# Weight decode and one of two r products moved to GpSimd in a fused recurrence and MLP kernel, with a refitted order of work

## The chip, the core and the metric

One NeuronCore of one Trainium2 chip runs the whole program. The metric is the device time of one execution in microseconds. Engines are named as in the profile: PE is TensorE, PEld its weight loads, DVE is VectorE, ACT is ScalarE, POOL is GpSimd, SP is SyncE, which issues nearly all DMAs.

## What is computed

A gated linear recurrence over 768 steps (4 batches, 8 heads of width 48) is followed by a two-layer MLP whose gate is a clipped parabola.

```python
for t in range(S):                      # S = 768
    cur = einsum('bhd,bhe->bhde', u[None] * kt, vt)
    y[:, :, t] = einsum('bhd,bhde->bhe', rt, state + cur)
    state = wt[:, :, :, None] * state + einsum('bhd,bhe->bhde', kt, vt)
x = y.transpose(0, 2, 1, 3).reshape(3072, 384)
h = x @ w_in                            # 384 x 2048
g = where(h >= 1, h, where(h <= -1, 0, (h + 1) ** 2 / 4))
out = g @ w_out                         # 2048 x 384
```

## The kernel before

**Units.** The recurrence is cut into 12 units `u` of 64 steps for all batches (256 tokens). A unit's channels lie in two tiles, `q` = 1 and 0. `attention(u)` loads w, r, k, v, makes the running product `p` of w by a scan on DVE (L550) and the running decay `y` backwards by a second scan (L545), multiplies k by `y` (L571) and r by `p` (L621), both on DVE. PE then forms the score matrices (`among`, L591), transposes k (L630), updates the state (`umat`, L660) and forms the output (`cross` and `along`, L703). These are matmuls of 64 rows, 64 to 192 in a run. In units 0 to 2 (`early`) the score's diagonal comes from a second `among` on `ku`, k times u, made by ACT (L561) from `rk` and a column of the constants tile `cst`. `picked` (L597) copies masked scores from PSUM on DVE. In later units POOL forms r times k (L609) and spreads the diagonal sums (L617). Units 0 and 1 also put the fourth pair of heads in place by matmuls with `perm` (L800); the others do it by small DMAs from `last` to `x`.

**Split numbers.** The products run on pairs of fp32r tiles, high part and remainder. For x of blocks 4 and 5 (`FLAT`) ACT first copies the output to `xf`, and `divided` then makes the high part (ACT, L1150) and the remainder (DVE, L1152) of each half block. For blocks 0 to 3 that is done out of PSUM, four pieces a unit, ACT L781 and DVE L779.

**Weights.** The 16 weight tiles arrive as 64-bit words. For each, ACT makes the scaled upper word `s` (L481) and the lower bits as 16-bit halves (L483); the sign goes into the other halves by `tensor_scalar` with a 16-bit strided output, on POOL for 13 tiles and on DVE for tiles 9, 10, 12 (L485). DVE joins them (L487), ACT rounds to the high part `w_hi` (L477; DVE in tiles 2 and 7, L475), DVE subtracts for `w_lo` (L490):

```python
on, e = ("DVE", V) if f in SIGNS else ("POOL", G)
op(on, 0.62 if f in SIGNS else 3.2, due, [("fl", k)], [("raw", f)], lambda: e.tensor_scalar(
    out=half(1), in0=s, scalar1=0.0, scalar2=32768.0, op0=ALU.is_lt, op1=ALU.mult))
```

**The MLP.** It runs in 6 blocks of 512 tokens and 16 steps `f`. Each step is 9 matmuls of `product_in` (L1369), the gate (ACT L1178, L1179, L1182; DVE L1180, L1183) and 9 matmuls of `product_out` (L1389). Blocks 3 to 5 use a scheme with fewer output products (L1045), for which DVE and POOL form sums of weights (L967). Blocks 0 and 1 begin in half blocks of 256 tokens.

**Order.** A planner (`Plan`) knows every operation's engine, cost in us and dependencies, simulates the engines, tries orders by shaken due times, and emits the instructions in the best order found; each engine then runs its own queue in that order. It marks operations with `port=True`, of which it lets only one run at a time on DVE and POOL together. Where it sees PE idle it puts in matmuls on a zero tile (L439), so that the clock stays up.

Of the kernel before, what the change touches and what calls it, by code (L numbers as in the profile page):

```python
# [44 lines left out]
FLAT = {NB - 2, NB - 1}  # L45
# [5 lines left out]
USE, SPAN, COLUMN = 0.68, 3.4, 0.00168  # L51

EAGER, LATE = 16.0, 0.3
RISES = 7.0
COLD = 7.0
# [3 lines left out]
BACK, SHAKES, SHAKE, SEED = 4, 40, 0.7, 5  # L59
# [4 lines left out]
class Plan:  # L64
# [10 lines left out]
    BLOCK, FETCH = 256, 3.9  # L75
# [12 lines left out]
    def add(self, engine, cost, emit, due, reads=(), writes=(), port=False, size=0, fresh=True, first=None, grab=False, uses=(), drop=None, code=0):  # L88
# [9 lines left out]
        self.ops.append(dict(e=engine, cost=cost, emit=emit, due=due, deps=deps, port=port, size=size,  # L98
                             fresh=fresh and engine == "PE", touch={*reads, *writes}, first=first, grab=grab, drop=drop, then=None, code=code,
                             uses={n} if grab else {*uses, *(() if drop is None else (drop,))}))  # L100
        return n
# [17 lines left out]
    def best(self, steps, times):  # L119

        found = None
        for _ in range(ROUNDS):
            for op in self.ops:
                when, ahead = op["due"]
                op["key"] = times[when] - ahead
            order = self.order()
            end = max(self.end.values())
            if found is None or end < found[0]:
                found = end, order, (self.begin, self.end, self.given, self.extra)
            times = [self.begin[n] for n in steps]  # L130

        draw = random.Random(SEED)
        for n in range(SHAKES):
            if n % BACK == 0:
                self.begin, self.end, self.given, self.extra = found[2]
            for op, key in zip(self.ops, self.late()):
                op["key"] = key + draw.gauss(0.0, SHAKE) * (n % BACK == 0 < n)
            order = self.order()
            end = max(self.end.values())
            if end < found[0]:  # L140
                found = end, order, (self.begin, self.end, self.given, self.extra)
        self.begin, self.end, self.given, self.extra = found[2]
        for op in self.ops:
            op["touch"] |= {("b", self.given[n]) for n in op["uses"]}
        return found[1]
# [39 lines left out]
    def kept_warm(self, order, engine, banks, fill):  # L185

        ops, begin, end = self.ops, self.begin, self.end
        free, out, busy = 0.0, [], []
        used = {b: [n for n in order if b in ops[n]["touch"]] for b in banks}
        for n in order:  # L190
            op = ops[n]
            if op["e"] == engine:
                at = begin[n]
                use = sum(max(0.0, y - max(x, at - SPAN)) for x, y in busy)
                lack = at - free - (0.3 if at > EAGER else -LATE if free < COLD else 0.1)
                if at > EAGER:
                    lack = min(USE * SPAN - use, lack)
                if free and lack > 0.15:
                    for b in banks:
# [4 lines left out]
                            ops[m]["e"] == engine for m in (before, after)) and end[before] <= free  # L204
                        fresh = after is None or ops[after]["fresh"]
                        if held or fresh and at - max(0.0 if before is None else end[before], free) > (lack if at > EAGER else at - free - 0.3 - 1e-6):
                            out.append(lambda b=b, lack=lack, free=free, held=held: fill(b, lack, free, held))
                            busy.append((at - lack, at))
                            break
                free = at + op["cost"]  # L210
                busy.append((at, free))
            out.append(op["emit"])
        return out

    def order(self):
# [18 lines left out]
        issued = [(0, -99.0, 0.0)]  # L234

        def fetched(code):
            at = issued[-1][0] + code - self.BLOCK
            for had, t, each in reversed(issued):
                if had <= at:
                    return t + (at - had) * each + self.FETCH  # L240
            return 0.0
# [4 lines left out]
        def ready(n):  # L246
# [3 lines left out]
            if ops[n]["code"] > 64:  # L250
                t = max(t, fetched(ops[n]["code"]) - ops[n]["cost"])
# [6 lines left out]
        while any(open_.values()):  # L258
            best = None
            for e, ns in open_.items():  # L260
# [10 lines left out]
            assert t < never  # L271
            n = min((n for n in open_[e] if ready(n) <= t + 1e-9 and forced.get(e) in (None, n)),
                    key=lambda n: (ops[n]["key"] if ops[n]["first"] is None else ops[n]["first"] - 1e3, n))
            op = ops[n]
            open_[e].remove(n)
            forced[e] = op["then"]
            if e == "PE":
                had = issued[-1][0]
                if op["code"]:
                    issued[-1] = had, t, op["cost"] / op["code"]  # L280
                    issued.append((had + op["code"], t + op["cost"], 0.0))
# [11 lines left out]
            end[n] = t + op["cost"] * (2 if e == "PE" and t < RISES else 1)  # L293
# [4 lines left out]
            if op["size"]:  # L298
                bus = max(bus, t) + op["size"] / (300e3 if t < 8.0 else 390e3)
                end[n] = bus + 2.0  # L300
# [46 lines left out]
SPLITS = {2, 7}  # L347
SIGNS = {9, 10, 12}
# [8 lines left out]
def attention_moe(tc, a):  # L357
# [17 lines left out]
    cst = one([128, 132 + C], F32, "cst", cpool)  # L375
    ident, twice, u_col = (cst[:, i:j] for i, j in ((0, 128), (128, 128 + C), (128 + C, 132 + C)))
# [10 lines left out]
    wq = tiles(3, [128, SEG + 1], F32, "wq")  # L387
# [18 lines left out]
    xf = tiles(len(FLAT), [128, 3, WIDE], F32, "xf")  # L406
# [27 lines left out]
    def zeros(to, n, add):  # L434

        while n >= 32:
            m = min(512, n if n < 128 else n // 128 * 128)
            rhs = zero[:, 0:m] if m <= 128 else zero.unsqueeze(1).broadcast_to([128, m // 128, 128])
            PE.matmul(to[:, 0:m], lhsT=zero, rhs=rhs, start=not add, stop=True, skip_group_check=add)  # L439
            n -= m  # L440
# [6 lines left out]
    op("PE", 3.0, SOON, ["zero"], [("b", b) for b in SPARE], warm)  # L447
# [4 lines left out]
    def weight(f, when):  # L452
# [7 lines left out]
        def front():  # L460

            return wraw[f].rearrange("p c two -> p (c two)")[:, 0:768]

        def half(i):
            return front().bitcast(U16).rearrange("p (c two) -> p c two", two=2)[:, :, i]
# [5 lines left out]
        def split():  # L471
            wt = wpool.tile([128, 2, 768], F32R, tag="wt", name=f"wt{f}")
            w_hi[f], w_lo[f] = wt[:, 0, :], wt[:, 1, :]
            if f in SPLITS:
# [12 lines left out]
        op("DVE", 0.97, due, [("raw", f), ("flight", f % FLIGHT)], [("fl", k)], lambda: V.scalar_tensor_tensor(  # L487
            out=s.bitcast(I32), in0=s.bitcast(I32), scalar=3, in1=front(), op0=ALU.logical_shift_left, op1=ALU.bitwise_or), port=True)
        op(*(("DVE", 0.48) if f in SPLITS else ("ACT", 0.83)), due, [("fl", k)], [("wh", f), ("raw", f)], split, port=f in SPLITS)
# [15 lines left out]
    def attention(u, when, lead=None):  # L505
        if u == EARLY:
            load((when, 40.0), u_sb, a["us"], ["us"])
# [18 lines left out]
        for q in (1, 0):  # L526
            load(due, wq[slot[q]], a["w"][u, q], [("w", slot[q])], first=rank(1 - q))
            load(due, rk[slot[q]], a["rk"][u, q], [("k", slot[q]), ("r", slot[q])], first=rank(4 - 2 * q))
        if u == 0:
            load(due, cst, a["consts"], ["cst"], first=3)  # L530
# [5 lines left out]
        if u == 0:  # L536
            load(due, perm, a["perm"], ["perm"], [vk])
# [20 lines left out]
        def with_u(q):  # L558
            for pr in range(2):
                cs = slice(pr * UT, pr * UT + UT)  # L560
                A.mul(ku[:, q, cs], rk[slot[q]][:, 1, cs], u_col[:, 2 * q + pr : 2 * q + pr + 1])  # L561

        for q in (1, 0):
            s = slot[q]
            if early:
                op("ACT", 1.0, due, [("k", s), "cst"], [("ku", q), "nk"], lambda q=q: with_u(q))
# [4 lines left out]
            op("DVE", 0.69, due, ["y"], [("k", s)], lambda q=q: V.tensor_tensor(  # L571
# [30 lines left out]
        if early:  # L602
            bd = [take(), take()]
            op("PE", 1.27, due, [("ku", 0), ("ku", 1), "nk", *both], [("b", bd[0]), ("b", bd[1])],
               lambda: among(bd, lambda q: ku[:, q]), code=128)
# [14 lines left out]
        for q in (1, 0):  # L620
            op("DVE", 0.69, due, [("p", q)], [("r", slot[q])], lambda q=q: V.tensor_tensor(  # L621
# [4 lines left out]
        def ktrans(q, b):  # L626
# [5 lines left out]
        op("PE", 1.27, due, [("k", slot[0]), ("k", slot[1]), *both], [("b", ba[0]), ("b", ba[1])],  # L632
           lambda: among(ba, lambda q: rk[slot[q]][:, 1]), code=128)
# [46 lines left out]
        def fade(g):  # L680
            V.tensor_tensor(out=heads(new, g), in0=heads(new, g), in1=faded(g), op=ALU.mult)
# [3 lines left out]
        def multiplied():  # L685
            return op("PE", 1.07 if glued else 1.27, due, [("kt", 0), ("kt", 1), vk], ukeys, umat, uses=lent.values(), code=128)

        def stepped():
            for g in range(2):
                op("DVE", 0.55, due, [ukeys[g], ("ptot", u, 0), ("ptot", u, 1)] + ([("s", old, g)] if u else []), [("s", new, g)],  # L690
                   lambda g=g: step(g), drop=lent[0] if glued and g else None)
                if u:
                    op("DVE", 0.57, due, [("ptot", u, 0), ("ptot", u, 1)], [("s", new, g)], lambda g=g: fade(g), port=True)
# [46 lines left out]
        if alone:  # L740
            op("PE", 0.5, due, ["zero"], [("b", by[0]), ("b", by[1])], cleared)
        run = []
        if u:
            run.append(op("PE", 0.64 if glued else 0.8, due, ss + [vk, ("r", slot[0]), ("r", slot[1])], [("b", by[0]), ("b", by[1])], cross, fresh=not alone,
                          grab=glued, code=64))
            if glued:
                lent[0] = run[0]
            for g in range(2):
                op("ACT", 0.15, due, [("b", by[g])], [("look", g)], lambda g=g: A.copy(look[0:1, g : g + 1], bank[by[g]][0:1, 0:1]))
# [709 lines left out]
```

## Time and profile before

| | |
|---|---|
| median of 3 runs | 501.91 us (501.64 to 502.25) |
| the profiled execution, its own time | 503.06 us |
| its span, first to last instruction | 501.5 us |
| mean granted TensorE clock | 0.993 |
| instructions of PE, DVE, ACT, POOL | 5767, 702, 658, 80 |

Busy time of PE counts overlapping matmuls and says little on how well PE is filled; the chain of work, in order of time, shows what each stretch waited for. A line of that chain has the start, the length and the engine, tile and line.

### The profile page before, as it was taken

To read this page: it belongs to the slowest core of one execution; us is meant where nothing else is said; L and a number is where in the kernel's file an instruction comes from. 1 tells how busy PE (TensorE), PEld (TensorE's weight loads), DVE (VectorE), ACT (ScalarE), POOL (GpSimd) and SP (SyncE) were. 2 spreads that over 40 slices of the span, in tenths; PEclk is the share of its full clock that TensorE was granted. 3 is DMA by queue.
4 is the path that set the end of the run, shared out by engine and by line. 5 is a ranking of instruction groups with operands and counts; after the bars stand their busy time and mean duration, and the time that the engine had idled before them with its cause. 6 is when DMAs were issued, how large, how long until landed. Compare 5 with 4: busy or idle time off the path is not lost.

```text
span 501.5 us, 13736 instructions
## 1 busy us (share of the span) xinstructions
PE 488.0 (97%) x5767; PEld 426.8 (85%) x5767; DVE 404.1 (81%) x702; ACT 312.7 (62%) x658; POOL 101.4 (20%) x80
## 2 busy tenths in 40 slices
PE   6979999999999999999999999999999999999996
PEld 4768988889999998888888788889899989898985
DVE  5899999988888898898999878779877675675573
ACT  4669799855555473765555656788866565465461
POOL 1656604530111111303031124432100000000000
PEclk9989999999999999999999999999999999999999
DMA  8984750522343434446153212222141000010002
GB/s 293 400 300 163 300 211 17 185 81 86 107 133 107 141 103 138 169 137 215 39 210 105 106 52 74 42 52 55 30 118 22 1 1 1 23 41 1 3 1 69
DMA packets 33286, 54.30 MB, mean 108 GB/s; under 512 B 15424, under 2 KB 22720, under 8 KB 33216
## 3 DMA queue, kind: packets, MB, share of 16 engines
q1 hardware_dynamic: 32784, 52.95, 31.9%
q8 instruction: 47, 0.77, 0.6%
q10 hardware_dynamic: 432, 0.39, 0.2%
q14 instruction: 23, 0.19, 0.1%
HBM read 47.04 MB, written 4.72 MB: 103 GB/s over the span
## 4 chain that ended last, share of the span: by engine, by line
PE 90%; DVE 4%; DMA 2%; issue 2%; ACT 1%; SPq 0%; DVEq 0%; ACTq 0%
PE h L1369 39%; PE acc L1389 20%; PE acc L1045 10%; PE bank L1045 9%; PE bank L703 4%; PE bank L591 3%; PE bank L630 2%; PE bank L660 1%; DMA cst<-in_consts 1%; DMA rk<-in_rk 1%; DVE fl L487 1%; PE bank L439 1%; PE acc L591 1%; DVE wt L490 1%; DVE y L545 0%
## 5 line engine op out<-in xcount | busy, mean ns | idle before, releaser
L1369 PE MATMUL h<-x,wt 128*128 128x512 f32 (+1 forms) x1035 | 220.1, 360 | 3.0 <-DVE x L779 2.9
L1369 PEld LDWEIGHTS h<-x,wt 128*128 128x128 f32 x1035 | 169.5, 189 | 31.7 <-DVE x L779 3.1
L1389 PE MATMUL acc<-gh,wt 128*128 128x256 f32 (+1 forms) x402 | 80.3, 335 | 0.0
L1389 PEld LDWEIGHTS acc<-gh,wt 128*128 128x128 f32 x402 | 60.9, 188 | 7.4
L1007 DVE SCALAR_TENSOR_TENSOR rk<-rk,h 128x512 f32<-128x512 f32 x48 | 32.8, 683 | 35.8 <-ACT rk L1006 34.2
L1178 ACT ACTIVATE g<-h 128x256 f32<-128x256 f32 (+1 forms) x67 | 31.9, 476 | 44.8 <-PE h L1369 40.6
L1004 ACT ACTIVATE rk<-h 128x512 f32<-128x512 f32 x48 | 28.6, 596 | 38.8 <-PE h L1369 38.8
L485 POOL TENSOR_SCALAR wraw<-fl 128x768 uint16<-128x768 f32 x13 | 41.8, 3224 | 51.4 <-ACT wraw L483 49.9
L1180 DVE SCALAR_TENSOR_TENSOR g<-g,h 128x256 f32<-128x256 f32 (+1 forms) x67 | 35.2, 529 | 14.4 <-ACT g L1179 12.4
L1389 PE MATMUL acc<-gl,wt 128*128 128x256 f32 (+1 forms) x201 | 44.5, 329 | 0.0
L1182 ACT CAST gh<-g 128x256 fp32r<-128x256 f32 (+1 forms) x67 | 32.7, 494 | 18.8 <-DVE g L1180 8.8
L617 POOL TENSOR_TENSOR r<-cst,d 128x512 f32<-128x512 f32 x18 | 20.2, 1143 | 99.8 <-PE bank L703 81.7
L1183 DVE TENSOR_TENSOR gl<-g,gh 128x256 fp32r<-128x256 f32 (+1 forms) x67 | 38.7, 589 | 0.8 <-ACT gh L1182 0.7
L1389 PEld LDWEIGHTS acc<-gl,wt 128*128 128x128 f32 x201 | 32.3, 188 | 4.0
L1179 ACT ACTIVATE g<-g 128x256 f32<-128x256 f32 (+1 forms) x67 | 34.4, 513 | 1.1
L550 DVE TENSOR_TENSOR_SCAN p<-wq,seeds 128x520 f32<-128x520 f32 x24 | 32.0, 1331 | 3.2 <-DMA wq<-in_w 2.3
L1006 ACT ACTIVATE rk<-rk 128x512 f32<-128x512 f32 x48 | 30.4, 634 | 0.9
L545 DVE TENSOR_TENSOR_SCAN y<-wq,seeds 128x520 f32<-128x520 f32 x24 | 29.8, 1242 | 0.8
L609 POOL TENSOR_TENSOR nk<-nk 128x768 f32<-128x768 f32 x9 | 17.3, 1920 | 61.4 <-DMA nk<-in_nk 37.9
L1013 DVE TENSOR_TENSOR gl<-rk,gh 128x512 fp32r<-128x512 f32 x36 | 25.5, 717 | 2.7 <-ACT gh L1012 2.4
L1013 DVE TENSOR_TENSOR g_again<-rk,nk_again 128x512 fp32r<-128x512 f32 x33 | 22.8, 701 | 5.8 <-ACT nk_again L1012 5.5
L1012 ACT CAST gh<-rk 128x512 fp32r<-128x512 f32 x36 | 22.1, 619 | 8.3 <-DVE rk L1007 4.7
(212 smaller groups left out, 914.5 us busy)
## 6 DMA issues: line engine op xcount, KB each, us to landing
rk<-in_rk SPq DMA_DIRECT2D x24, 512.0 KB, 5.3
wraw<-in_wbits SPq DMA_DIRECT2D x16, 768.0 KB, 7.5
nk<-in_nk SPq DMA_DIRECT2D x9, 768.0 KB, 4.7
wq<-in_w SPq DMA_DIRECT2D x24, 260.5 KB, 2.9
vn<-in_v SPq DMA_DIRECT2D x12, 384.0 KB, 6.8
last<-in_w SPq DMA_DIRECT2D x12, 256.0 KB, 3.0
out_y<-xf SPq DMA_DIRECT2D x15, 128.0 KB, 1.8
out_y<-g SPq DMA_DIRECT2D x6, 256.0 KB, 2.2
```

The source lines that it names most:

```text
L485: op(on, 0.62 if f in SIGNS else 3.2, due, [("fl", k)], [("raw", f)], lambda: e.tensor_scalar(out=half(1), in0=s, scalar1=0.0, scalar2=327 ...
L550: V.tensor_tensor_scan(out=pv[:, q].rearrange("p n c -> p (n c)"), data0=w[:, 0:SEG], data1=sv, initial=0.0, op0=ALU.mult, op1=ALU.add,)
L1007: op("DVE", 0.66, due, [("h", n)], [qk], lambda: V.scalar_tensor_tensor(out=gf, in0=gf, scalar=1.0, in1=bank[plan.given[hk]], op0=ALU.min, ...
L1013: op("DVE", 0.67, due, [key, ("h", i, k)], fresh_in(("l", i, k)), lambda: V.tensor_tensor(out=spare(k, 3 + i), in0=x, in1=spare(k, i).bitc ...
L1045: PE.matmul(bank[i][:, half * UT : half * UT + UT], lhsT=w[wi], rhs=g[gi], start=(b, i) not in opened, stop=True, skip_group_check=True)
L1178: op("ACT", c, due, [("h", n)], [("g", gk)], lambda: nc.scalar.activation(gs, hs(), AF.Relu, scale=0.5, bias=0.5), uses=[hk])
L1179: op("ACT", c, due, (), [("g", gk)], lambda: nc.scalar.activation(gs, gs, AF.Square))
L1180: op("DVE", 0.13 + 0.53 * k, due, [("h", n)], [("g", gk)], lambda: nc.vector.scalar_tensor_tensor(out=gs, in0=gs, scalar=1.0, in1=hs(), op ...
L1182: op("ACT", c, due, [("g", gk)], [("gh", gk)], lambda: nc.scalar.copy(ghs, gs))
L1183: op("DVE", 0.17 + 0.54 * k, due, [("g", gk), ("gh", gk)], [("gl", gk)], lambda: nc.vector.tensor_tensor(out=gls, in0=gs, in1=ghs.bitcast( ...
L1369: nc.tensor.matmul(hp, lhsT=wx[f][:, cs], rhs=xt[:, j, :], start=n == 0, stop=n == 8)
L1389: nc.tensor.matmul(o[j], lhsT=wx[f][:, cs], rhs=gt, start=first and i == 0, stop=stop and i == 2, skip_group_check=True)
```

## The change

Weight signs: POOL multiplies `s` by zero in float32, which leaves the sign bit alone in a whole word `z`; ACT then writes the lower bits into the low halves of `z`. All 16 tiles do so. `z` lives in `xf[0]`, two places in turn. The high part of tiles 4 to 15 is copied on POOL, of tiles 0 to 3 on ACT. In every unit r times `p` for `q` = 0 runs on POOL. u's columns ride with the tile of w rather than with `cst`, which is loaded after both `rk`; `perm` is built by POOL from the identity rather than loaded. Blocks 1 to 5 are `FLAT`. The planner gets other costs, models PE's instruction loading, prefers to keep runs of 64-row matmuls together (`HOLD`), repeats its fill of idle PE time on a replayed order, and applies a list of seeded local shakes (`MOVES`).

```diff
-FLAT = {NB - 2, NB - 1}
+FLAT = set(range(1, NB))
-USE, SPAN, COLUMN = 0.68, 3.4, 0.00168
+USE, SPAN, COLUMN = 0.68, 3.4, 0.00184
-RISES = 7.0
-COLD = 7.0
+RISES = COLD = 6.0
-BACK, SHAKES, SHAKE, SEED = 4, 40, 0.7, 5
+BACK, SHAKES, SHAKE, SEED = 4, 12, 0.7, 3
+MOVES = (475382, 526387, 473247, 945916, 280867, 888496, 655704, 241438, 861928, 885623, 756977,)
...
+    BLOCK, EDGE, LEAD, DENSE = 256, 194, 3, 1 / 700
+    FETCH, BUSY, SLOWER = 3.75, 45.0, 5.0
+    SWITCH, HOLD, LOOK = 0.125, 0.25, 30.0
...
+            if e == "PE" and pe["small"] and forced.get(e) is None:
+                n = min((n for n in open_[e] if ops[n]["small"] and ready(n) <= t + self.HOLD), key=lambda n: (ready(n), n), default=None)
+                if n is not None:
+                    t = max(t, ready(n))
...
-SPLITS = {2, 7}
-SIGNS = {9, 10, 12}
+SPLITS = set()
+SPARED = set(range(4, NF))
+SIGN, HALF = 1.0, 1.08
+SPREAD, SHARED = {(i, 0) for i in range(NU)}, set()
...
+            if f in SPARED:
+                G.tensor_copy(w_hi[f], s)
...
-        op("ACT", 1.09, due, (), [("raw", f)], lambda: A.activation(half(0), words(0, U32), AF.Copy, scale=LOW))
-        on, e = ("DVE", V) if f in SIGNS else ("POOL", G)
-        op(on, 0.62 if f in SIGNS else 3.2, due, [("fl", k)], [("raw", f)], lambda: e.tensor_scalar(
-            out=half(1), in0=s, scalar1=0.0, scalar2=32768.0, op0=ALU.is_lt, op1=ALU.mult))
+        op("POOL", SIGN, due, [("fl", k)], [zk], lambda: G.tensor_scalar(out=z, in0=s, scalar1=0.0, scalar2=None, op0=ALU.mult))
+        op("ACT", 1.09, due, [("raw", f), ("flight", f % FLIGHT)], [zk], lambda: A.activation(low_half(), words(0, U32), AF.Copy, scale=LOW))
...
-        op(*(("DVE", 0.48) if f in SPLITS else ("ACT", 0.83)), due, [("fl", k)], [("wh", f), ("raw", f)], split, port=f in SPLITS)
+        op(*(("POOL", HALF) if f in SPARED else ("DVE", 0.48) if f in SPLITS else ("ACT", 0.83)), due, [("fl", k)], [("wh", f), ("raw", f)], split, port=f in SPLITS and f not in SPARED)
...
-            load(due, cst, a["consts"], ["cst"], first=3)
+            load(due, cst, a["consts"], ["cst"], first=4)
...
-            load(due, perm, a["perm"], ["perm"], [vk])
+            op("POOL", 0.4, due, [], ["perm"], lambda: G.memset(perm, 0.0))
+            for j in range(3):
+                op("POOL", 0.2, due, ["cst"], ["perm"], lambda j=j: G.tensor_copy(
...
-                A.mul(ku[:, q, cs], rk[slot[q]][:, 1, cs], u_col[:, 2 * q + pr : 2 * q + pr + 1])
+                A.mul(ku[:, q, cs], rk[slot[q]][:, 1, cs], wq[slot[q]][:, SEG + 1 + pr : SEG + 2 + pr])
...
-            op("DVE", 0.69, due, [("p", q)], [("r", slot[q])], lambda q=q: V.tensor_tensor(
+            on, e = (("POOL", 1.15), G) if (u, q) in SPREAD else (("DVE", 0.69), V)
+            op(*on, due, [("p", q)], [("r", slot[q])], lambda q=q, e=e: e.tensor_tensor(
                 out=parts(q, 0), in0=parts(q, 0), in1=pv[:, q, :, 0:C], op=ALU.mult), port=True)
...
-        op("PE", 1.27, due, [("k", slot[0]), ("k", slot[1]), *both], [("b", ba[0]), ("b", ba[1])],
-           lambda: among(ba, lambda q: rk[slot[q]][:, 1]), code=128)
+        op("PE", 0.95, due, [("k", slot[0]), ("k", slot[1]), *both], [("b", ba[0]), ("b", ba[1])],
+           lambda: among(ba, lambda q: rk[slot[q]][:, 1]), code=128, small=True)
...
+                if u % 2 and u // 2 in FLAT and u // 2 < NB - 2:
+                    divided(u // 2)
```

## Rows read from the trace of the kernel before

**Rows 1.** The page's first part: busy time of each engine, share of the span, instructions.

```profile
PE 488.0 (97%) x5767; PEld 426.8 (85%) x5767; DVE 404.1 (81%) x702; ACT 312.7 (62%) x658; POOL 101.4 (20%) x80
```

**Rows 2.** Stretches of the span: length, then busy time of PE, PEld, DVE, ACT and POOL with the instructions started in brackets, granted clock, share of the DMA engines, GB/s.

```profile
0.00:60.00 60.00, 51.79 (x950) 43.45 (x951) 51.92 (x81) 40.77 (x83) 30.27 (x23) 0.94 0.78 285
60.00:100.00 40.00, 40.00 (x381) 33.57 (x380) 37.46 (x55) 35.11 (x61) 15.57 (x6) 1.00 0.44 158
100.00:120.00 20.00, 20.00 (x156) 16.50 (x154) 17.07 (x29) 9.25 (x19) 3.93 (x3) 1.00 0.28 91
120.00:310.00 190.00, 190.00 (x3101) 165.68 (x3098) 165.79 (x297) 109.18 (x274) 36.14 (x30) 1.00 0.37 122
310.00:496.60 186.60, 186.18 (x1190) 167.62 (x1188) 131.48 (x243) 118.38 (x224) 15.48 (x20) 1.00 0.12 29
496.60:501.50 4.90, 0.00 (x0) 0.00 (x0) 0.42 (x1) 0.00 (x0) 0.00 (x0) 1.00 0.28 85
```

**Rows 3.** The chain of work that ended last, in order of time, from 0 to 62 us: start, length, engine, tile, line.

```profile
2.36 5.36 DMA cst<-in_consts
7.81 0.92 ACT nk L561 x2
...
41.00 0.67 ACT wt L477
...
44.01 4.09 DMA rk<-in_rk
...
56.91 0.57 DVE rk L621
...
57.53 1.16 PE bank L591 x64
58.69 1.26 PE h L1369 x9
```

**Rows 4.** The same chain between 189 and 211 us, where it is PE alone.

```profile
189.03 2.10 PE h L1369 x9
...
192.69 2.29 PE h L1369 x9
...
205.48 0.62 PE bank L703 x32
...
207.03 2.30 PE h L1369 x9
209.32 1.56 PE bank L703 x96
210.88 2.28 PE h L1369 x9
```

**Rows 5.** Waits of DVE in the first 60 us: who waited for whom, us in total, times, longest.

```profile
DVE r L597 <- PE bank L591: 1.7, 2, 1.1
...
DVE rk L621 <- PE acc L591: 0.7, 1, 0.7
DVE rk L571 <- ACT nk L561: 0.6, 1, 0.6
DVE fl L487 <- POOL wraw L485: 0.4, 1, 0.4
```

**Rows 6.** Groups of instructions by line: engine, operation, tiles, shapes, count, busy us, mean ns of one, idle time before them. The row of L621 is of the first 100 us alone, and so is that of L475; the last line is one of the order of time (start, length).

```profile
L485 POOL TENSOR_SCALAR wraw<-fl 128x768 uint16<-128x768 f32 x13 | 41.8, 3224 | 51.4 <-ACT wraw L483 49.9 <-DMA rk<-in_rk 1.5
L609 POOL TENSOR_TENSOR nk<-nk 128x768 f32<-128x768 f32 x9 | 17.3, 1920 | 61.4 <-DMA nk<-in_nk 37.9 <-DVE y L545 12.8 <-PE acc L1389 10.7
L617 POOL TENSOR_TENSOR r<-cst,d 128x512 f32<-128x512 f32 x18 | 20.2, 1143 | 99.8 <-PE bank L703 81.7 <-issue 18.0
L477 ACT CAST wt<-fl 128x768 fp32r<-128x768 f32 x14 | 11.7, 833 | 3.1 <-DVE fl L487 3.1
L621 DVE TENSOR_TENSOR rk<-rk,p 128x512 f32<-128x512 f32 x6 | 3.9, 679 | 0.7 <-PE acc L591 0.7
L475 DVE CAST wt<-fl 128x768 fp32r<-128x768 f32 x2 | 1.1, 546 | 0.0
L485 DVE TENSOR_SCALAR wraw<-fl 128x768 uint16<-128x768 f32 x3 | 1.8, 616 | 0.0
L779 DVE TENSOR_TENSOR x<-bank,x 128x384 fp32r<-128x384 f32 x14 | 7.5, 549 | 2.0 <-ACT last L781 1.9
L1152 DVE TENSOR_TENSOR x<-xf,x 128x768 fp32r<-128x768 f32 x4 | 3.8, 950 | 0.0
1.60 0.98 POOL L429 MEMSET r<- 128x512 f32 x2
```

**Rows 7.** The order of time on DVE and on POOL, around 53 us and around 111 us: start, length, engine, line, operation, tiles, shapes, count.

```profile
52.74 3.02 POOL L485 TENSOR_SCALAR wraw<-fl 128x768 uint16<-128x768 f32 x1 [5.21 <-ACT wraw L483]
...
53.01 1.10 DVE L571 TENSOR_TENSOR rk<-rk,y 128x512 f32<-128x512 f32 x1
54.03 0.41 DVE L1183 TENSOR_TENSOR gl<-g,gh 128x256 fp32r<-128x256 f32 x1
54.37 0.94 DVE L490 TENSOR_TENSOR wt<-fl,wt 128x768 fp32r<-128x768 f32 x1
...
110.83 1.85 POOL L609 TENSOR_TENSOR nk<-nk 128x768 f32<-128x768 f32 x1 [2.62 <-DMA nk<-in_nk]
...
111.66 1.57 DVE L1183 TENSOR_TENSOR gl<-g,gh 128x512 fp32r<-128x512 f32 x1 [0.74 <-ACT gh L1182]
```

More of the change, by code (lines that the diff above doesn't have):

```diff
@@ L86, in __init__, with add @@
         self.given, self.extra = {}, {}
-    def add(self, engine, cost, emit, due, reads=(), writes=(), port=False, size=0, fresh=True, first=None, grab=False, uses=(), drop=None, code=0):
+    def add(self, engine, cost, emit, due, reads=(), writes=(), port=False, size=0, fresh=True, first=None, grab=False, uses=(), drop=None, code=0, small=False, look=False):
         deps = {self.writer[x] for x in (*reads, *writes) if x in self.writer}
@@ L119, in best @@
     def best(self, steps, times):
-        found = None
+        self.put_in, self.found = {}, None
         for _ in range(ROUNDS):
[L123 to L129, printed above, removed]
+            self.attempt([times[op["due"][0]] - op["due"][1] for op in self.ops])
             times = [self.begin[n] for n in steps]
@@ L208, in kept_warm @@
-                            busy.append((at - lack, at))
+                            columns = int((lack - max(0.0, min(at, COLD) - free) / 2) / COLUMN)
+                            if columns >= 32:
+                                out[n] = b, columns, held, 4 * len(self.pieces(columns))
+                                busy.append((at - lack, at))
                             break
-                free = at + op["cost"]
+                free = end[n]
                 busy.append((at, free))
-            out.append(op["emit"])
@@ L213, in kept_warm, with pieces, lands, records @@
         return out
+    def pieces(self, n):
+        out = []
+        while n >= 32:
+            out.append(min(512, n if n < 128 else n // 128 * 128))
+            n -= out[-1]
+        return out
+    def lands(self, bus, t, size):
+        bus = max(bus, t) + size / next(rate for until, rate in self.RATES if t < until)
+        return bus, bus + self.WAY
+    def records(self, n):
+        return self.put_in[n][-1] if n in self.put_in else 0
+    def pe_takes(self, n, t, pe, between=0.0):
+        op = self.ops[n]
+        idle = self.records(n)
+        was = pe["small"] and not idle
+        cost = op["cost"] + self.SWITCH * (op["small"] != was) + self.EVENT * op["code"]
+        for code, start, span in ((idle, between, t - between), (op["code"] * (1 + self.DENSE), t, cost)):
+            past = -(pe["count"] - self.EDGE) % self.BLOCK
+            if past < code:
+                at = start + span * past / code
+                when = pe["edge"] + (self.SLOWER if at < self.BUSY else self.FETCH)
+                if start == t:
+                    cost += max(0.0, when - at)
+                pe["edge"] = max(at, when)
+            pe["count"] += code
+        pe["small"] = op["small"]
+        return cost
@@ new lines, in replay @@
+    def replay(self, order):
+        ops = self.ops
+        free, end, begin, lands = {}, {}, {}, []
+        port = bus = 0.0
+        pe = dict(count=self.LEAD, edge=-99.0, small=False)
+        for n in order:
+            op = ops[n]
+            e = op["e"]
+            t = max((end[m] + self.after(m, n) for m in op["deps"]), default=0.0)
+            if n in self.extra:
+                t = max(t, end[self.extra[n]] + self.HOPS[ops[self.extra[n]]["e"]])
+            t = max(t, free.get(e, 0.0))
+            if op["port"]:
+                t = max(t, port)
+            if op["size"] and len(lands) >= LANES:
+                t = max(t, lands[-LANES])
+            cost = op["cost"]
+            if e == "PE":
+                cost = self.pe_takes(n, t, pe, free.get(e, 0.0)) * (2 if t < RISES else 1)
+            begin[n], end[n] = t, t + cost
+            free[e] = end[n] - self.OVERLAP.get(e, 0.0)
+            if op["port"]:
+                port = free[e]
+            if op["size"]:
+                bus, end[n] = self.lands(bus, t, op["size"])
+                lands.append(end[n])
+        self.begin, self.end = begin, end
@@ L233, in order @@
         forced, given, extra = {}, {}, {}
[L234 to L241, printed above, removed]
+        pe = dict(count=self.LEAD, edge=-99.0, small=False)
         spare = [(0.0, b, None) for b in SPARE]
@@ L249, in ready @@
                 t = max(t, min(spare)[0]) if spare else never
-            if ops[n]["code"] > 64:
-                t = max(t, fetched(ops[n]["code"]) - ops[n]["cost"])
+            if ops[n]["small"]:
+                past = -(pe["count"] + self.records(n) - self.EDGE) % self.BLOCK
+                m, took = n, 0.0
+                while m is not None:
+                    code = ops[m]["code"] * (1 + self.DENSE)
+                    if past < code:
+                        when = pe["edge"] + (self.SLOWER if t < self.BUSY else self.FETCH)
+                        return max(t, when - took - ops[m]["cost"] * past / code)
+                    past, took, m = past - code, took + ops[m]["cost"], ops[m]["then"]
             return t
@@ L692, in stepped @@
                 if u:
[L693 removed]
+                    op(*(("POOL", 0.9) if (u, g) in FADED else ("DVE", 0.57)), due, [("ptot", u, 0), ("ptot", u, 1)], [("s", new, g)], lambda g=g: fade(g), port=True)
         begun = set()
```

192 lines of the change are left out of this document (114 added, 78 removed).

## The prediction

> **What bounds the kernel now.** I first read the engines' busy shares, and there PE seems to be everything, 97% of the span [rows 1]. That number does not tell where time can be won, because overlapping matmuls keep it high even when PE is badly filled. So the second view is the table of stretches. It shows two kernels in one: in the first 60 us DVE is busy 51.92 us and PE runs only 950 of its 5767 matmuls, and from 60 us on PE is busy without a break to 496.6 us [rows 1, 2]. The third view, the chain of work in order of time, puts the border precisely. Until 57.5 us the chain goes through a DMA (5.36 us to the constants, 4.09 us to an rk tile), through ACT and mostly through DVE; its last DVE piece is L621 at 56.91 us, and at 57.53 us PE takes it over [rows 3]. Sampled further on, between 189 and 211 us, it is PE after PE [rows 4]. Behind the last matmul stand 4.9 us of one addition and the last stores [rows 2].
>
> So two things can shorten the time. One is an earlier point at which PE takes the chain over; 57.5 us stand there, mostly DVE's. The other is less time in PE's own stream of about 439 us (496.6 less 57.5). The change deletes no matmul of the products, so in that stream only the joints can give: nine 512-column matmuls take 2.10 us behind others of their kind, and 2.28 to 2.30 us next to a run of 64-row matmuls [rows 4]. A change of sort costs about 0.19 us. I count three runs in each of the nine later units (the scores; the cross part with the state update; the output), 27 x 0.19 = 5.1 us in all.
>
> Anything taken off DVE, ACT or POOL after 57.5 us is worth nothing while PE stays supplied.
>
> **The change part by part, up to 57.5 us.**
>
> *The start of unit 0.* DVE waits three times before 17 us: 0.6 us for ku on ACT, which itself waits for the constants, then 0.7 and 1.1 us for PE's score runs, both behind ku; together 2.4 us [rows 3, 5]. With u's columns in the tile of w, ku no longer needs the constants, and an earlier weight tile can fill the remaining holes. The rk tile that ku needs may land hardly earlier than the constants did, so the lower end is 0 and the upper 2.4; I take 1.5, as the two later waits are also holes that a ready weight tile can fill.
>
> *r times p.* Units 0, 1 and 2 do both products before 57.5 us; L621 is the last DVE piece of the chain [rows 3]. Three instructions of 0.679 us leave DVE [rows 6]: 2.0 us. On POOL each takes about what L617, same shape and two inputs, takes, 1.14 us [rows 6]. The score run needs both products, so the POOL one is hidden beside DVE's own 0.68 us and other work; if the cover is gone the scores come 0.5 us later per unit.
>
> *The high part of tile 2* leaves DVE, 0.55 us [rows 6]. Tile 7 and the three DVE signs (0.62 us each, rows of the same group) lie after the border or near it; I price them at nothing, hidden behind PE.
>
> *POOL's signs.* 3.22 us become a float32 pass over 768 columns. No such row exists: from below a pure write (two memsets of 512 columns in 0.98 us, so about 0.75 us for 768), from above two inputs at that size, 1.92 us [rows 6]. I take 1.1 us, nearer to the write, as there is one input. Each tile's chain gets some 2 us shorter. But DVE has a queue of other work there and waited for a sign only 0.4 us in the first 60 us [rows 5]. So the sum gets 0.4, not 2 us per tile. The sign now comes before ACT's lower bits, so ACT can stall on POOL; with 0.4 us as the wait in the other direction I leave that at nothing and keep up to 1 us for the range.
>
> *High parts on POOL.* ACT loses 0.83 us for each of tiles 4 and 5 in this stretch and gains one for tile 2 [rows 6]. The chain runs through ACT's L477 at 41.0 us for 0.67 us [rows 3]; I count 0.7 us, between 0 and 1.7.
>
> *What POOL takes from DVE.* POOL's own instructions delay DVE's. At 111.66 us L1183 took 1.57 us while L609 ran from 110.83 to 112.68 us; at 53.01 us L571 took 1.10 us, beside L485 that had begun at 52.74 us [rows 7]. Against the 0.68 us that two such 128x512 inputs take in L621 [rows 6], that is 0.9 and 0.4 us. The bounds for each new POOL pass are nothing (DVE happens to read PSUM, or waits anyway) and the whole pass, 1.1 us for r times p and up to 1.9 us for a copy. For five of them before the border (three products, two copies) I take 0.36 us each, near the 0.4 us of the 53 us row: 1.8 us lost; the ends are 0 and 7.2 us. The signs delayed DVE before as well, and I let that stand as it is.
>
> Here a rule speaks against the change. The Trainium skill, page "SBUF — State Buffer", section "Who interferes with whom", says that a VectorE instruction with two SBUF inputs and a GpSimd instruction that reads SBUF shut each other out for the whole instruction of whichever began first. The row at 111 us agrees: L1183 ended 0.55 us after L609. The row at 53 us does not: L571, L1183 and L490 all finished by 55.31 us, inside L485's run to 55.76 us, the last two in 0.41 and 0.94 us [rows 7]. By the rule each old sign would have cost DVE 3 us and its replacement would win back most of that, some 12 us over six tiles; by the row it wins next to nothing, and the sum goes by the row.
>
> *FLAT for blocks 1 to 3.* Four DVE pieces out of PSUM per unit (the two large ones 0.55 us each) become one of 0.95 us per half block [rows 6], with ACT's copy ahead of it. All of it falls behind the border, where PE has its work; the cover is DVE's 5.5 us of idle time between 60 and 120 us [rows 2]. Building perm on POOL takes a DMA out of the queue and puts four short passes into POOL's, before tile 0's sign; nothing.
>
> **In PE's stream.** `HOLD` can join the output run to the state update of the same unit when its inputs are ready, one joint less in a unit: at most 9 x 0.19 = 1.7 us. I take 1.0. What the other planner costs and the seeds do to the order beyond this cannot be read from rows; I put 0 and keep 1 us either way.
>
> **The sum.** 1.5 + 2.0 + 0.55 + 0.4 + 0.7 - 1.8 + 1.0 = 4.35 us. The profiled execution took 503.06 us, 1.56 us more than its span, and 1.15 us more than the median of the runs. 503.06 - 4.35 = 498.7 us in its own terms, 497.6 us against the median; I forecast 497.5 us. With every term at its good end it is 2.4 + 2.0 + 0.55 + 0.4 + 1.7 + 1.7 + 1 = 9.8 us, 492 us.
>
> **The rivals.**
>
> *PE's start moves much further*, because the new order uses the shorter weight chains as well: the good ends above, 491 to 494 us. For it speaks that the PE clock share is 0.94 in the first 60 us and that only 950 matmuls run there [rows 2]; against it that DVE's work there, 51.9 us, shrinks by only 2.6 us.
>
> *No change*: the locks give back what leaves DVE. Five new passes at 0.9 us (the 111 us row) cost 4.5 us, against 1.5 + 2.0 + 0.55 + 0.4 + 0.7 = 5.15 us won: 501.3 us before the joints, and within 1 us of 501.9 if those give nothing.
>
> *Slower: POOL's copies starve PE between 60 and 105 us.* Eleven or so tiles are decoded after the border begins to matter, and the planner does not count the copy as excluding DVE (`port` is false for it). DVE is busy 37.46 of 40 us from 60 to 100 us, and there are 5.5 us of slack up to 120 us [rows 2]; 3 signs, a split and a product per unit leave DVE there, some 4 us. Ten copies that each hold DVE for more than 0.95 us would use up these 9.5 us. At the full 1.9 us of a two-input pass they cost 19 us, and PE would stand some 9 us: minus the 4.35, about 506.5 us. Against it: at 53 us the delay was 0.4 us.
> By the rule of the Trainium skill's page "SBUF — State Buffer" (section "Who interferes with whom") a copy would hold DVE for all of its length whenever DVE comes second, which is this rival's mechanism.
>
> **How the numbers follow.** I give the forecast case (1 to 7 us won) 0.55, the far start 0.20, no change 0.13, slower 0.12. One measurement of this kernel tells about 0.2%, 1 us. The predicted time is that of the likeliest case. The range from 492 to 503 us takes in the far start, no change and the mild part of the slower case. The likeliest case's own range is 495 to 501 us. Faster gets 0.75, the same 0.13, slower 0.12.
>
> **What would show it.** In the changed profile the chain should hand over to PE at about 54 us in place of 57.5 us, with the DMA of the constants gone from its beginning; PE should run without a break from there. L485 should take about 1.1 us, the copies on POOL about the same, r times p 1.1 us on POOL. DVE's two-input passes beside them should be stretched by some 0.4 us. Fewer pieces of 2.28 us should stand in the chain after 100 us. The prediction is wrong if PE waits for DVE or for weights after 60 us, if POOL's float32 passes are as slow as the old sign, or if the handover does not move or moves by more than 8 us.

## The result, and the profile after

The changed kernel takes 507.1 us (506.97 to 507.94) against 502.1 us before: ratio 1.0099, 95% interval 1.0076 to 1.0122. It is slower by 5 us, where 497.5 us with a range of 492 to 503 us had been forecast. The profiled execution took 507.06 us, its span 505.5 us, 4.0 us more than the span before.

The stretches of the span of the changed kernel (columns as in [rows 2]); the last row is a short stretch with the lower clock:

```profile
0.00:60.00 60.00, 45.38 (x869) 39.31 (x870) 49.57 (x74) 39.69 (x81) 33.85 (x34) 0.97 0.79 289
60.00:100.00 40.00, 36.87 (x417) 30.59 (x416) 35.40 (x48) 27.53 (x50) 25.42 (x16) 0.96 0.42 151
...
310.00:500.60 190.60, 190.51 (x1292) 171.43 (x1284) 133.37 (x248) 123.15 (x235) 17.95 (x23) 1.00 0.13 33
500.60:505.50 4.90, 0.00 (x0) 0.00 (x0) 0.37 (x1) 0.00 (x0) 0.00 (x0) 0.95 0.25 80
...
96.00:99.50 3.50, 3.50 (x10) 2.76 (x11) 3.47 (x5) 2.49 (x5) 2.47 (x1) 0.60 0.00 0
```

Against [rows 2], DVE fell in the first 60 us (51.92 to 49.57 us) and from 60 to 100 us (37.46 to 35.40), as the change meant it to. POOL rose between 60 and 100 us, from 15.57 to 25.42 us. And PE, full in that stretch before, now has holes: 36.87 of 40 us. It is less busy in the first 60 us too, 45.38 us against 51.79. The tail is the same 4.9 us.

The chain of work in order of time, from its start to 71 us:

```profile
1.87 5.61 DMA rk<-in_rk
7.57 0.92 ACT nk L677 x2
...
27.12 2.92 POOL xf L595
...
34.61 2.31 POOL xf L595
...
43.53 2.34 POOL xf L595
...
57.04 2.14 POOL xf L595
59.18 0.86 POOL wt L585
60.04 2.10 POOL xf L595
...
67.06 2.34 PE h L1489 x9
69.40 2.12 PE acc L1509 x18
```

and from 81 to 102 us:

```profile
81.16 0.43 DVE st L796
...
89.84 2.86 POOL xf L595
92.70 0.02 issue
92.72 1.08 ACT xf L596
93.80 0.02 issue
93.82 0.97 DVE fl L597
94.79 0.05 issue
94.84 0.84 POOL wt L585
95.68 0.08 issue
95.76 3.73 PE h L1489 x9
99.49 2.10 PE acc L1509 x9
```

[Rows 3] had no POOL piece among those shown, and PE took the chain over at 57.53 us. Here the sign pass (now L595) stands in the chain again and again, PE does not take over until 67.06 us, and it loses the chain once more, at 81.16 us: one whole weight tile (sign, lower bits, join, copy) stands in it in a row from 89.84 to 95.68 us. PE runs out of other work at 93.19 us and waits, and its next nine matmuls take 3.73 us. Behind a wait at full clock nine of them took 2.34 us (at 67.06 us); here the granted clock was 0.60, most of the stretch at the lower of the two levels, 1.2 GHz. The wait that ended was this one, from PE's list of waits:

```profile
PE h L1489 <- POOL wt L585: 2.6, 1, 2.6
```

So the two losses there are 2.6 us of waiting and 3.73 - 2.34 = 1.4 us of slow clock. The first handover came 9.5 us later than before, yet the span grew by 4.0 us only: from 67.06 us to the last matmul are 433.5 us with these losses in them, where 439.1 us stood behind the handover before. More of PE's work had been done by then, so the handover by itself does not measure the time.

The instructions on POOL, by groups (the first 106 us):

```profile
L595 POOL TENSOR_SCALAR xf<-fl 128x768 f32<-128x768 f32 x16 | 39.2, 2451 | 17.6 <-ACT fl L593 16.6 <-ACT look L867 1.0
L585 POOL CAST wt<-fl 128x768 fp32r<-128x768 f32 x12 | 11.8, 981 | 10.9 <-DVE fl L597 10.9
L739 POOL TENSOR_TENSOR rk<-rk,p 128x512 f32<-128x512 f32 x4 | 5.0, 1254 | 10.6 <-PE bank L708 5.3 <-PE acc L1509 4.4 <-PE acc L708 0.9
```

A copy of a weight tile takes POOL 0.98 us; a multiplication by a constant at the same size takes 2.45 us. The planner had 1.0 us for it, the forecast 1.1. ACT, which writes the lower bits (L596) into the words that the sign pass has made, stood 15.4 us waiting for it, in 12 waits:

```profile
L596 ACT ACTIVATE xf<-wraw 128x768 uint16<-128x768 uint32 x16 | 17.3, 1082 | 15.4 <-POOL xf L595 15.4
```

In the kernel before it was POOL that waited for ACT's lower bits (49.9 us, first line of [rows 6]).

### The profile page after: what moved, and what is told of

Its sections match the earlier page's. It is cut to its first block, busy times and chain, and to the rows that moved or that the text cites. A ratio compares the mean times of both kernels' runs of the same rounds, so it can differ in the third digit from the quotient of the medians.

```text
span 505.5 us, 13662 instructions
## 1 busy us (share of the span) xinstructions
PE 482.8 (96%) x5747; PEld 424.0 (84%) x5747; DVE 399.1 (79%) x667; ACT 311.1 (62%) x654; POOL 128.9 (26%) x111
## 4 chain that ended last, share of the span: by engine, by line
PE 85%; issue 4%; POOL 4%; ACT 3%; DVE 2%; DMA 1%; SPq 0%; POOLq 0%; DVEq 0%; ACTq 0%
PE h L1489 37%; PE acc L1509 18%; PE acc L1163 10%; PE bank L1163 9%; PE bank L821 4%; POOL xf L595 3%; PE bank L708 2%; PE bank L748 2%; PE bank L778 1%; DMA rk<-in_rk 1%; ACT xf L596 1%; DVE fl L597 1%; POOL wt L585 1%; PE acc L708 1%; DVE gl L1302 0%
## 5 line engine op out<-in xcount | busy, mean ns | idle before, releaser
L1302 DVE TENSOR_TENSOR gl<-g,gh 128x256 fp32r<-128x256 f32 (+1 forms) x67 | 43.8, 671 | 4.8 <-ACT gh L1300 4.7
L595 POOL TENSOR_SCALAR xf<-fl 128x768 f32<-128x768 f32 x16 | 39.2, 2451 | 17.6 <-ACT fl L593 16.6
L734 POOL TENSOR_TENSOR r<-cst,d 128x512 f32<-128x512 f32 x18 | 21.3, 1201 | 67.2 <-PE bank L821 50.4
L666 DVE TENSOR_TENSOR_SCAN p<-wq,seeds 128x520 f32<-128x520 f32 x24 | 30.4, 1268 | 3.2 <-DMA wq<-in_w 2.1
L596 ACT ACTIVATE xf<-wraw 128x768 uint16<-128x768 uint32 x16 | 17.3, 1082 | 15.4 <-POOL xf L595 15.4
```

Of the source, the lines that this page charges most:

```text
L595: op("POOL", SIGN, due, [("fl", k)], [zk], lambda: G.tensor_scalar(out=z, in0=s, scalar1=0.0, scalar2=None, op0=ALU.mult))
L666: V.tensor_tensor_scan(out=pv[:, q].rearrange("p n c -> p (n c)"), data0=w[:, 0:SEG], data1=sv, initial=0.0, op0=ALU.mult, op1=ALU.add,)
L1302: op(*on, due, [("g", gk), ("gh", gk)], [("gl", gk)], lambda: e.tensor_tensor(out=gls, in0=gs, in1=ghs.bitcast(F32), op=ALU.subtract), por ...
```

## The experiments

The theories: **S**, the sign pass is over twice as long as the planner thinks, so POOL is late with the weights; **L**, POOL's new passes shut DVE out; **R**, r times p on POOL delays the scores; **O**, the refitted order is worse in itself. The first five runs keep the order of every other instruction of the changed kernel and alter one line of the code, an operation or its engine. Each ratio is to the kernel before on the same chip, with its 95% interval.

**A memset for the sign.**

```diff
-lambda: G.tensor_scalar(out=z, in0=s, scalar1=0.0, scalar2=None, op0=ALU.mult))
+lambda: G.memset(z, 0.0))
```

> The changed kernel in its own order, with one instruction replaced: POOL's sign pass, which multiplies a tile by zero (L595, 16 of them, mean 2.45 us in the changed kernel's trace where the planner counted 1.0), becomes a memset of the same 128x768 words, about 0.8 us. The weights' signs are left out of the computation. Theory S (the sign pass is over twice as long as planned, so POOL hands the weight tiles out late and PE starves between 45 and 100 us): the 6 us lost there come back, 499 to 502 us. Theory L (the new POOL passes shut DVE out): the copies still do that, 504 to 507 us. Theory R (r times p on POOL delays the scores): 506 to 508 us. Theory O (the refitted order itself is worse): 506 to 508 us.

Measured: 499.5 us, 0.9946 (0.9924 to 0.9969). The pass took 0.74 us:

```profile
L595 POOL MEMSET xf<- x16: 735/740/746, 13.2 to 90.4; 128x768 f32 x16
```

ACT's waits for it shrink from 15.4 us to one of 0.4 us (in all, and how often):

```profile
  ACT xf L596: 0.4, 1
```

All that the change lost, and 2.6 us more, hangs on this one instruction in this one order. R and O fall: r times p and the order were as in the changed kernel. L remains possible in part, since a memset does not read.

**A copy for the sign.**

```diff
+lambda: G.tensor_copy(z, s))
```

> The changed kernel in its own order, POOL's sign pass replaced by a plain copy of the same 128x768 float32 words on POOL: it reads and writes as the sign pass does, but should take about 0.9 us as POOL's other copies do. The words are then not signs but whole numbers, so the weights are wrong in this run. It parts two readings of the memset run (499.5 us). Theory S (the length of the pass counts): 499 to 501 us. Theory L2 (reading SBUF on POOL beside DVE counts, which a memset doesn't do): 503 to 507 us.

Measured: 503.0 us, 1.0016 (0.9995 to 1.0037): outside S's bounds and at the lower end of L2's. The copy took 1.07 us in the median, and ACT waited for it less than for the sign pass, but more than for the memset:

```profile
  ACT xf L596: 3.9, 5
```

DVE's subtraction for `w_lo` (L600) between 40 and 106 us may show what a pass that reads does beside it; first the changed kernel, then the copy, then the memset:

```profile
L600 DVE TENSOR_TENSOR wt<-fl,wt 128x768 fp32r<-128x768 f32 x12 | 13.1, 1094 | 0.0
```

```profile
L600 DVE TENSOR_TENSOR wt<-fl,wt 128x768 fp32r<-128x768 f32 x12 | 13.1, 1091 | 0.1
```

```profile
L600 DVE TENSOR_TENSOR wt<-fl,wt 128x768 fp32r<-128x768 f32 x12 | 11.9, 995 | 0.1
```

The means differ by few instructions: with the sign pass and with the copy three of the twelve took 1.51 to 1.58 us, with the memset one, and the others 0.93 to 0.96 us. With the high-part copies on ACT and the sign pass as it was (a run below) the mean is 996 ns too, so the mean depends on which instructions the order puts side by side, and not on the sign pass alone.

So 507.1 less 503.0, some 4 us, go with the length of the pass from 2.45 to about 1.1 us, and the other 3.5 us with what is left: 0.3 us of length, and the reading. How these last two divide stays open. The copy is about as long as the forecast had the sign pass, and still the time is 5.5 us above the forecast.

**The sign on DVE, same place.**

```diff
+lambda: V.tensor_scalar(out=z, in0=s, scalar1=0.0, scalar2=None, op0=ALU.mult))
```

> The changed kernel in its own order, the float32 sign pass issued to DVE at the same place of the order instead of to POOL; the whole computation is kept. DVE gets 16 passes of some 0.6 us, 9.6 us in the first 100 us, and POOL loses 39 us. Theory S: DVE is nearly full there, but the 6 us of starvation go; 500 to 504 us. Theory L or O: DVE pays 9.6 us and nothing comes back but the locks of the sign passes, 507 to 511 us.

Measured: 505.2 us, 1.0061 (1.0037 to 1.0085), 2 us under the changed kernel and a little above what S gave. A pass takes DVE 0.55 us in the median:

```profile
L595 DVE TENSOR_SCALAR xf<-fl x16: 527/550/2171, 14.7 to 96.0; 128x768 f32<-128x768 f32 x16
```

DVE is busy 38.41 of 40 us between 60 and 100 us there, and ACT still waits 4.9 us for the sign. That DVE is too full for 16 more passes in this order is likely, but not shown.

**The copies on ACT, same place.**

```diff
-G.tensor_copy(w_hi[f], s)
+A.copy(w_hi[f], s)
```

> The changed kernel in its own order, the 12 copies of high parts issued to ACT at the same place instead of to POOL (0.83 us each there in the kernel before). The sign passes stay on POOL. Theory L: 501 to 503 us. Theory S: POOL's queue shortens by 0.95 of some 3.4 us a tile, ACT gets busier; 503 to 507 us. Theories R and O: 506 to 509 us.

Measured: 506.4 us, 1.0079 (1.0049 to 1.0109), within S's bounds, at the edge of R's and O's, and far from L's. Moving the copies, on which the forecast's slower rival rested, off POOL gives back some 0.7 us, which does not stand clear of the intervals.

**r times p on DVE, same place.**

```diff
-on, e = (("POOL", 1.15), G) if (u, q) in SPREAD else (("DVE", 0.69), V)
+on, e = (("POOL", 1.15), V) if (u, q) in SPREAD else (("DVE", 0.69), V)
```

> The changed kernel in its own order, r times p for q = 0 issued to DVE at the same place instead of to POOL, in all 12 units. Theory R: 502 to 505 us. Theory S: POOL has 1.2 us less in each of the four early units, DVE 0.68 us more; 506 to 508 us. Theories L and O: 506 to 508 us.

Measured: 508.1 us, 1.0115 (1.0083 to 1.0147), where R had 502 to 505 us. R falls here too.

**The true price in the planner.** The next runs alter no instruction but the order.

```diff
-SIGN, HALF = 1.0, 1.08
+SIGN, HALF = 2.3, 0.9
```

with another list in `MOVES`.

> The changed kernel with nothing but the planner's prices mended: 2.3 us for the sign pass in place of 1.0, 0.9 for the copy in place of 1.08, and a list of shakes found anew for these prices. The instructions are the same, the order differs. If the price was the fault (the order starves because it was planned for a pass of 1 us), 498 to 502 us. If the instruction is (POOL at 2.3 us a sign cannot deliver in time in any order), 504 to 507 us.

Measured: 502.0 us, 0.9991 (0.9970 to 1.0013): 5 us under the changed kernel and the same as before. The pass is no shorter, but PE no longer waits for a copy of POOL (L585), ACT waits for the sign 1.7 us in place of 15.4, and PE is nearly full between 60 and 100 us:

```profile
L595 POOL TENSOR_SCALAR xf<-fl x16: 2128/2470/3064, 12.0 to 93.4; 128x768 f32<-128x768 f32 x16
```

```profile
  ACT xf L596: 1.7, 5
```

```profile
60.00:100.00 40.00, 39.65 (x430) 32.80 (x429) 39.02 (x50) 30.86 (x54) 30.18 (x17) 1.00 0.45 168
```

**Its control: the old price, a fresh order.** As above with `SIGN, HALF = 1.0, 0.9`, and its own list.

> The control to the run with mended prices (502.0 us): the same instructions and the same kind of fresh shakes, and the copy at 0.9 us there too, but the sign pass priced at 1.0 us again. If the price of the sign was the fault, 505 to 508 us, as the changed kernel. If any fresh order would have done, 501 to 503 us.

Measured: 506.8 us, 1.0089 (1.0063 to 1.0115). A fresh order with the wrong price is as slow as the changed kernel, and ACT waits for the sign as long again (its profiled execution, at 509.28 us, was the longest of its six):

```profile
60.00:100.00 40.00, 37.99 (x424) 31.57 (x425) 35.76 (x46) 25.94 (x47) 25.90 (x15) 1.00 0.45 164
100.00:120.00 20.00, 18.23 (x77) 13.81 (x76) 18.60 (x28) 10.86 (x19) 4.47 (x5) 1.00 0.10 22
```

```profile
L596 ACT ACTIVATE xf<-wraw 128x768 uint16<-128x768 uint32 x16 | 17.4, 1088 | 19.0 <-POOL xf L595 19.0
```

So 4.7 us, 506.8 less 502.0, go with one number in the planner. The two lists of shakes differ as well, each found for its own price; but both orders at the wrong price took about 507 us, and the five runs at 2.3 us, here and below, 500.5 to 502.2 us. At the wrong price ACT's instructions come where the sign is not yet done, and the weights come late.

**Only the weight part undone.**

```diff
-op("POOL", SIGN, due, [("fl", k)], [zk], ...)
+on, e = ("DVE", V) if f in SIGNS else ("POOL", G)
+op(on, 0.62 if f in SIGNS else 3.05, due, [("fl", k)], [("raw", f)], ...)
```

with the lower bits, the join, `SIGNS` and `SPLITS` as before the change, and `SPARED` empty.

> All of the change except its weight part: the signs go into 16-bit halves again (13 on POOL at a planned 3.05 us, tiles 9, 10, 12 on DVE), high parts on ACT and DVE as before; r times p, FLAT, the loads and the planner as changed, with shakes found anew. If the gains lie in the rest of the change and the weight part only loses, 497 to 500 us, below every run so far with real signs. If the float32 sign is worth something at its real 2.1 to 2.4 us, 501 to 504 us, above the runs with mended prices.

Measured: 501.4 us, 0.9985 (0.9967 to 1.0003): the time lies in the second range, but below the run with mended prices (502.0 us), not above it, and the two cannot be told apart. The 16-bit sign takes POOL 3.37 us here, almost 1 us more than the float32 one, and does no harm where the planner knows it:

```profile
L599 POOL TENSOR_SCALAR wraw<-fl 128x768 uint16<-128x768 f32 x13 | 43.6, 3366 | 26.6 <-ACT wraw L597 22.7 <-DMA wq<-in_w 3.7 <-POOL nk L730 0.3
```

The weight part is worth nothing that can be measured, and the rest of the change gains at most 0.3%.

**Where to put what, at the true price.** `SPARED` empty (all copies on ACT); `SPARED` from tile 10; `SPARED` empty and the float32 signs of tiles 9, 10, 12 on DVE; `SPARED` and `SPREAD` empty. Each has its own list.

> As the run with mended prices, and all copies of high parts back on ACT; its own shakes. POOL then has the sign passes and r times p alone. If POOL's queue is the bound, 496 to 500 us, below the run with mended prices. If DVE or ACT is the bound by then, 500 to 503 us.

> As the run with mended prices, with the copies of tiles 4 to 9 back on ACT and those of tiles 10 to 15 on POOL; its own shakes. If POOL is the bound early and ACT later, this is the best of the three, 496 to 500 us; if the copies hardly matter, as the run with all copies moved in the old order suggests, the three lie within 2 us of each other.

> As the run with mended prices and all copies on ACT (500.8 us), with the float32 signs of tiles 9, 10 and 12 issued to DVE (0.55 us each as measured there) and shakes found anew: the last third of the weights, where POOL was latest, is relieved. If POOL is still what is late, 498 to 500 us; if DVE is, 501 to 503 us.

> As the run with mended prices and all copies on ACT (500.8 us), with both products of r and p on DVE again and shakes found anew. It prices the moved product: 0.68 us of DVE in each of the three or four units before the border. If the product is worth what the forecast gave it, 502 to 504 us; if POOL's hold on DVE gives it back, 500 to 502 us.

| run | us | ratio to before (95%) |
|---|---|---|
| copies on ACT | 500.8 | 0.9974 (0.9952 to 0.9995) |
| copies on ACT up to tile 9 | 500.8 | 0.9959 (0.9946 to 0.9972) |
| copies on ACT, three signs on DVE | 500.5 | 0.9966 (0.9949 to 0.9982) |
| copies on ACT, no r times p on POOL | 502.2 | 0.9993 (0.9972 to 1.0015) |

The first three are 0.3 to 0.4% quicker than the kernel before and by the ratios 1.2 to 1.4% quicker than the changed kernel. They cannot be told apart from each other, nor surely from the run with all late copies on POOL, which had 502.0 us; the three placements of copies lie within 2 us of each other, as the second expectation had it. Three signs on DVE gave 500.5 us, between the two ranges expected. With both products on DVE the time is 1.4 us worse than with one on POOL, where the forecast's 2.0 us less three holds of 0.36 us are 0.9 us; the intervals overlap, so this is inconclusive.

## Why the prediction was wrong, point by point

**What bounds the kernel: right in its two parts, wrong in where they meet.** The loss fell before and just as PE took the chain for good, at 95.76 us, and every run that was quicker than the kernel before filled PE nearly fully between 60 and 100 us (39.2 to 40.0 of 40). But the forecast counted on PE staying supplied from the handover on, and here it did not: the 2.6 us wait for a weight tile after 60 us is one of the signs of being wrong that the forecast had named. The tail stayed at 4.9 us.

**The step that failed: POOL's signs.** The forecast priced the pass at 1.1 us, "nearer to the write, as there is one input", between two memsets and a two-input product at 1.92 us [rows 6]. It measured 2.45 us, and 2.13 us at its shortest, above the upper bound. The nearest row was another: the old sign, the same operation with a constant, at 3.22 us [rows 6]. An operation with a constant was judged by its number of inputs rather than by its kind.

From that came the second part of the same step: "the sum gets 0.4, not 2 us per tile", since DVE had waited for a sign only 0.4 us [rows 5]. That holds for a kernel whose order had been planned with 3.2 us for that pass. It says nothing for an order planned with 1.0 us. The forecast took a wait from the old order into a new one, and did not ask what the planner's own price would do if it was wrong. Between the control and the true price, for the same instructions, lie 4.7 us.

The forecast saw the place: "The sign now comes before ACT's lower bits, so ACT can stall on POOL". It left that at nothing and kept up to 1 us for the range. ACT stood there 15.4 us in 12 waits, 19.0 us in the control, and 1.7 us where the planner had the true price. DVE's own wait in the first 60 us, 0.4 us for the sign before, became 2.2 us for the lower bits that now follow it:

```profile
DVE fl L597 <- ACT xf L596: 2.2, 2, 1.2
```

**What this step does not explain.** The miss is 9.6 us, 507.1 less 497.5. With a pass of 1.07 us in the same order (the copy) the time was 503.0 us, and with the true price 502.0 us, so the sign accounts for four to five of them. The other half is the gain of 4.35 us that did not come: no run that keeps the signs was more than about 2 us quicker than the kernel before. Which of the terms failed there stays open, but for what follows.

**The start of unit 0: too much.** 1.5 us had been taken of 0 to 2.4. The DMA of the constants has left the chain, but the rk tile stands in its place (5.61 us from 1.87 us), ku starts at 7.57 in place of 7.81 us, and DVE's waits are in all what they were:

```profile
DVE r L714 <- PE bank L708: 1.4, 2, 1.1
DVE r L714 <- PE acc L708: 1.0, 1, 1.0
...
DVE rk L688 <- ACT nk L677: 0.6, 1, 0.6
```

That is 3.0 us, as the first three such waits of [rows 5] are (1.7, 0.7 and 0.6 us); the forecast's 2.4 us are those before 17 us, 2.7 us now. By these waits the lower end, 0, would have been right.

**r times p: sized right on POOL** (1.25 us against 1.14), and DVE's busy time before 60 us fell by 2.35 us. The forecast had 2.0 + 0.55 us. The gain could not be shown by itself.

**What POOL takes from DVE: right in kind.** Between 84 and 90 us of the changed kernel, first POOL, then DVE:

```profile
85.35 1.50 POOL L585 CAST wt<-fl 128x768 fp32r<-128x768 f32 x1 [1.74 <-DVE fl L597]
86.82 5.87 POOL L595 TENSOR_SCALAR xf<-fl 128x768 f32<-128x768 f32 x2
```

```profile
85.21 0.94 DVE L600 TENSOR_TENSOR wt<-fl,wt 128x768 fp32r<-128x768 f32 x1
86.12 0.07 DVE L665 MEMSET seeds<- 128x8 f32 x1
86.22 1.72 DVE L666 TENSOR_TENSOR_SCAN p<-wq,seeds 128x520 f32<-128x520 f32 x1
87.86 1.51 DVE L600 TENSOR_TENSOR wt<-fl,wt 128x768 fp32r<-128x768 f32 x1
89.29 0.19 DVE L660 RECIPROCAL seeds<-p 128x8 f32<-128x8 f32 x1
```

The copy that began during L600 took 1.50 in place of 0.82 us, and the scan behind it 1.72 in place of 1.24. The second L600 took 1.51 us in place of 0.94. The hold works both ways, and its 0.5 to 0.7 us each time are somewhat more than the 0.36 us that the forecast had taken; the sum over all passes was not measured. The second L600 began and ended within POOL's two sign passes, 86.82 to 92.69 us. Ten microseconds earlier another L600 ran within a sign pass that had begun before it, and neither was stretched:

```profile
75.93 2.13 POOL L595 TENSOR_SCALAR xf<-fl 128x768 f32<-128x768 f32 x1
```

```profile
76.84 0.94 DVE L600 TENSOR_TENSOR wt<-fl,wt 128x768 fp32r<-128x768 f32 x1
```

The Trainium skill's rule (page "SBUF — State Buffer", section "Who interferes with whom") of a lock for the whole instruction is therefore not borne out for the constant pass, as [rows 7] had it; that a pass which only writes does not contend agrees with the memset run, where all 16 passes took 0.735 to 0.746 us, while the copies took 0.825 to 1.774 us.

**The joints.** Behind 57 us the order of time on PE has 26 changes from runs of scores, state updates and outputs to other matmuls, 30 before. At 0.19 us each that is 0.8 us, near the 1.0 us of the forecast; the price of one is unchanged (2.29 to 2.30 us beside 2.10 in the chain around 200 us).

**The rivals.** "Slower" was given 0.12 and 506.5 us; the time came close, by another mechanism. Its copies cost some 0.7 us in this order (the run with copies on ACT), not 19 us. "The planner does not know the real length of what it places" was not among the rivals, though the diff held the planner's price in plain sight beside a row that spoke against it.

## What to carry to other kernels

Where a planner writes the order, a wrong cost in it can cost more than the instruction (here 4.7 us, where the same pass at its true price cost nothing that could be measured): check each new price in a diff against the nearest row of the same operation, not of the same shape. A wait that was short in the old order is no evidence for the new one. To part an instruction from the order around it, keep the order and exchange the one instruction; then keep the instruction and mend only its price, with a control that has the wrong price and a fresh order.

## What the runs showed of the hardware

On POOL, at 128x768 float32, a memset took 0.74 us, a copy 0.82 us at its shortest, a product of two inputs 1.84 us, and a multiplication of one input by a constant 2.13 us at its shortest: the operation with a constant was the slowest of them, though it reads one tile. DVE does the same multiplication in 0.55 us. Beside a POOL pass that reads, DVE's subtraction took 0.93 to 0.96 us most times and 1.51 to 1.58 us at others (changed kernel and copy run, 40 to 106 us). The longer time was the same beside the copy as beside the sign pass, which takes twice as long; what decides between the two times is not shown.
